# The second block's second product by seven half-size products, and a start-up that loads the second pair's v first

## The chip, the cores and the metric

The kernel runs on one core of a Trainium2 chip. Its time is the device time of one execution in microseconds (us); several executions are measured, and the median counts. A core has five engines that run their own instruction streams in order and meet at semaphores: TensorE (PE in the profile; its weight loads are PEld) multiplies matrices into the PSUM buffers, VectorE (DVE) and ScalarE (ACT) work elementwise and move PSUM to SBUF, GpSimd (POOL) works on SBUF and issues some DMAs, SyncE (SP) issues the other DMAs. DMA queues move data between HBM and SBUF.

## The reference

Two layers, one after the other, over 4 sequences of 768 tokens (3072 tokens), 8 heads of 64 dimensions:

```python
state = np.zeros((B, H, D, D))
for t in range(S):
    state = gamma * state + outer(k[:, :, t], v[:, :, t])   # per head, gamma = 1 - 2**(-5 - h)
    y[:, :, t] = scale * q[:, :, t] @ state                 # scale = 1 / sqrt(D)
x = y as [3072 tokens, 512]
h = np.maximum(x @ w_in, 0.0)                               # w_in 512 x 2048
out = (h * h) @ w_out                                       # w_out 2048 x 512
```

All inputs and the output are float32; the kernel multiplies in bfloat16 and accumulates in float32.

## The kernel before

The recurrence is done in 24 chunks of 128 tokens: scores of a chunk (queries against keys, masked), its outputs (scores against v, plus queries against the state so far), and the state carried on in PSUM. Decay is put into scaled copies of q, k and v. The first four chunks are done as two pairs (`scores_pair`, `outputs_pair`, `state_pair`, `finish_pair`): pair 0 is chunks 0 and 1, pair 2 is chunks 2 and 3. Chunks 4 to 7 go through `scale_q`, `scale_kv`, `transpose_k`, `scores`, `state`, `outputs`; from chunk 8 on a packed form with DMA transposes is used (`scores2` and so on).

The feed-forward layer works on blocks of chunks: `BLOCKS` gives the first block four chunks, and ten more blocks two chunks each. Its first product (L846, `first_product`) has 128-column weights of w_in as the stationary side; ScalarE takes the relu out of PSUM (L855), VectorE squares it (L826). For the second product there are two ways:

- the plain one (`second`, L1175, stored by L1185 and L1187): 16 matmuls of 512 columns for each chunk;
- `seven_products` (L880 for its matmuls, L876 for its sums): the block's 256 tokens, the 2048 inner values and the 512 output columns are halved each, and the product is made of seven half-size products (each eight matmuls of 256 columns) of sums s1 to s4 of parts of h and t1 to t4 of parts of w_out (L341, `sum_w_out`). Its last product, with s4, is kept back and run in the next block, between that block's units (`kept`).

Before the change blocks 2 to 10 use seven products, block 1 the plain way. Block 0 uses the plain way for its first two chunks and seven products for its last two, in `last_of_first` (L1000 for the sums, L1004 and L1039 for the matmuls). There `u` is a sum that VectorE makes from the first finished products and that must be made before the third product (s3 with t3) goes on in the same buffer; s3 is made by `third_sums`, s4 by `fourth_sums`.

Nothing is scheduled automatically. Each engine runs its instructions in the order in which the program issues them, and that order is written by hand: the start-up is a list of calls (from `keep_awake(10, ...)` to `load_kv(4, "k")`), and after it the blocks' work is cut into pieces; `put(n, what)` issues a step after piece n. Block 0's pieces are 5 to 32 (5 to 16 its first product, 17 to 32 its second), block 1's are 33 to 48, and each later block has pieces of its own after them. `attend(m, scaled, places)` puts the steps of chunk m: the scaling of q at `scaled`, then at the five places q's turning and k's scaling, k's turning, the first scores, the second scores and the state, the outputs.

In the start-up SP issues the loads in the order of the calls: q and k of the first chunks, the first pair's v, the first half of w_in's group 0, the second pair's v, the second half of w_in's group 0, and so on. Weights of w_in arrive in float32 and are cast by several engines (`cast_w`; its letters name the engines for the four parts: G is GpSimd, V VectorE, S ScalarE). `first_unit(0, 0, c, (part,))` runs half of the first product's group 0 for chunk c, eight matmuls of 128 columns. `keep_awake` runs matmuls on zeros while data is awaited.

PSUM buffers are given out by pools: `ps_f` has four buffers that are used in turn, `ps_tp`, `ps_st`, `ps_y` and `ps_c` one each. A new tile waits until the last use of the buffer's former tile is over.

Of the kernel before, what the change touches and what calls it, by code (L numbers as in the profile page):

```python
# [9 lines left out]
FP32 = mybir.dt.float32  # L10
BF16 = mybir.dt.bfloat16
# [13 lines left out]
PACK_FROM = 8  # L25


SEVEN = range(2, 11)


@with_exitstack
def kernel(
# [14 lines left out]
    C = 128  # L47
# [142 lines left out]
    load_pair(0, "kn", k, raw_k, heads_of[1])  # L190
    load_pair(2, "kn", k, raw_k)
    load_pair(0, "vn", v, raw_v)
    load_w_in(0, parts=2, between=lambda: load_pair(2, "vn", v, raw_v))
    load_w_in(1, parts=2)
    for g in range(2, NQ):
        load_w_in(g)
# [657 lines left out]
    def relu(hv, hp, on_scalar=False):  # L854
        nc.scalar.activation(hv, hp[:], AF.Relu)  # L855
        squares.append((hv, on_scalar))
# [3 lines left out]
    def seven_products(tb):  # L860
# [4 lines left out]
            t.rearrange("s p hh d -> s (p hh d)").rearrange("s (j t) -> s j t", t=C)  # L865
            for t in (k_bds[0], k_bds[1], v_bds[0])
        )
        s3 = a21
        t1, t2, t3, t4 = sums
        b11, b21, b22 = (  # L870
# [21 lines left out]

        def rest():
            first_sums(slice(4, 8))
            pa = ps_tp.tile([P, HN], FP32, name="tp")
            pb, pe, pd = (ps_f.tile([P, HN], FP32, name="psf") for _ in range(3))
            oa, ob = (opool.tile([P, DM], FP32, name="osb") for _ in range(2))
            a, u, v = (upool.tile([P, HN], FP32, name=f"u{i}") for i in range(3))
            r0 = first[tb] * C
            for js, stop in ((range(0, 6), False), (range(6, 8), True)):  # L900
                product(pa[:], a11, b11, js, True, stop)
                product(pe[:], a22, t4, js, True, stop)
                if stop:
                    nc.scalar.activation(a[:], pa[:], AF.Copy)
                yield
            add(s3, a11, a21, ALU.subtract)
            product(pd[:], s1, t1, range(8), True, True)
            yield
            add(s4, a12, s2, ALU.subtract)
            product(pb[:], s2, t2, range(8), True, True)  # L910
            add(u[:], pb[:], a[:])
            yield
            for js in (range(0, 4), range(4, 8)):
                product(pa[:], a12, b21, js, False, js[-1] == 7)
                if js[0]:
                    nc.scalar.activation(oa[:, 0:HN], pa[:], AF.Copy)  # L916
                yield
            for js in (range(0, 4), range(4, 8)):
                product(pb[:], s3, t3, js, False, js[-1] == 7)
                if js[0]:  # L920
                    add(v[:], pb[:], a[:])
                    add(ob[:, HN:DM], pd[:], v[:])
                    add(ob[:, 0:HN], pe[:], v[:])

                    def last_product():
                        product(pd[:], s4, b22, range(8), False, True)
                        add(oa[:, HN:DM], pd[:], u[:])
                        yield
                        nc.sync.dma_start(out[r0 + C : r0 + 2 * C], ob[:])
                        yield  # L930
                        nc.sync.dma_start(out[r0 : r0 + C], oa[:])
                        yield

                    kept.append(last_product())
                yield
# [167 lines left out]
    def first_unit(tb, g, c, parts=(0, 1)):  # L1103

        if tb not in h2s:
            h_tiles(tb)
        if (tb, g, c) not in open_ps:
            open_ps[tb, g, c] = ps_f.tile([P, FPQ, C], FP32, name="psf")
        hp = open_ps[tb, g, c]
        cols = slice(c * C, (c + 1) * C)  # L1110
        half = FPQ // 2
        for part in parts:
            for fq in range(part * half, (part + 1) * half):
                first_product(tb, hp[:, fq, :], g * FPQ + fq, cols)
        if 1 in parts:
            relu(h_of(tb, g * FPQ, (g + 1) * FPQ)[:, :, cols], open_ps.pop((tb, g, c)))

    def ffn_pieces(tb):
        nch = BLOCKS[tb]
        TB = nch * C  # L1120
        if tb == 0:
            first_sums, last_sums, second_products = last_of_first()
            put(11, first_sums, 0)
            put(17, first_sums, 1)
            put(26, last_sums[0])
            put(27, last_sums[1])
            for f in range(FPQ, NFB):
                hp = ps_f.tile([P, TB], FP32, name="psf")
                first_product(tb, hp[:], f, slice(0, TB))
                relu(h_of(tb, f)[:, 0], hp)  # L1130
                yield
            yield from second_products()
            return
        elif tb <= 2:

            for c in range(nch):
                for g in range(NQ):
                    first_unit(tb, g, c)
                    if c * NQ + g in (1, 2, 3) and kept:
                        next(kept[0])  # L1140
                    if c * NQ + g == 4:
                        kept.clear()
                    if tb in SEVEN and (c, g) == (1, 3):
                        first_sums, rest = seven_products(tb)
                        first_sums(slice(0, 4))
                    yield
            if tb in SEVEN:
                yield from rest()
                return
        else:  # L1150
            h_tiles(tb)
            per = 512 // TB
            if tb in SEVEN:
                first_sums, rest = seven_products(tb)
            for f0 in range(0, NFB, per):
                hp = ps_f.tile([P, per, TB], FP32, name="psf")
                for f in range(f0, f0 + per):
                    first_product(tb, hp[:, f - f0, :], f, slice(0, TB))
                relu(h_of(tb, f0, f0 + per), hp, tb in SEVEN and f0 // per in (1, 3))
                if f0 // per in (1, 2, 3) and kept:  # L1160
                    next(kept[0])
                if f0 // per == 4:
                    kept.clear()
                if f0 // per == 5 and tb in SEVEN:
                    first_sums(slice(0, 4))
                yield
            if tb in SEVEN:
                yield from rest()
                return


        def second(op, j, g, cols=slice(0, DM)):
            for fq in range(FPQ):
                f = g * FPQ + fq
                nc.tensor.matmul(  # L1175
                    op[:],
                    lhsT=h_of(tb, f)[:, 0, j * C : (j + 1) * C],
                    rhs=w_out_bf[g][:, fq, cols],
                    start=(f == 0),
                    stop=(f == NFB - 1),  # L1180
                )

        def store(op, j, cols=slice(0, DM)):
            osb = opool.tile([P, DM], FP32, name="osb")
            nc.scalar.activation(osb[:, cols], op[:], AF.Copy)  # L1185
            r0 = (first[tb] + j) * C
            nc.sync.dma_start(out[r0 : r0 + C, cols], osb[:, cols])  # L1187


        for j in range(nch):  # L1190
            op = ps_f.tile([P, DM], FP32, name="psf")
            for g in range(NQ):
                second(op, j, g)
                if g == NQ - 1:
                    store(op, j)
                yield
# [33 lines left out]
    transpose_pair_k(2, 1, *f)  # L1230
    cast_pair_v(0, 0)
    cast_pair_v(0, 1)
    mask_a = scores_pair(2, 0, (st, f), spare[:, 0:1024])
    keep_awake(2)
    end_awake()
# [4 lines left out]
    outputs_pair(0, 1)  # L1240
    mask_b = scores_pair(2, 1, (tp, f), spare[:, 1024:2048])
    mask_b(0)
    mask_b(1)
    finish_pair(0, 0)
    finish_pair(0, 1)
    state_pair(0, 1, "SV")
    cast_w("in", 0, (0,), "GGGG")
    cast_pair_v(2, 0)
    cast_pair_v(2, 1, on_scalar=True)
    first_unit(0, 0, 0, (0,))  # L1250
    first_unit(0, 0, 1, (0,))
    cast_w("in", 0, (1,), "GGVV")
    outputs_pair(2, 0, ((ps_y, "y"), st))
    outputs_pair(2, 1)
    finish_pair(2, 0)
    state_pair(2, 0, "VV")
# [23 lines left out]
    def attend(m, scaled, places):  # L1280
        if m % 2 == 0:
            put(scaled, scale_q, m, 0)
            put(scaled + 2 if m == 4 else scaled, scale_q, m, 1)
            put(places[0], transpose_q, m)
        put(16 if m == 4 else places[0], scale_kv, m)
        put(places[1], transpose_k, m)
# [27 lines left out]
    put(20, sum_w_out, 0)  # L1314
    put(22, sum_w_out, 1, (0, 1), slice(0, 2))
    put(24, sum_w_out, 1, (0, 1), slice(2, 4))
    put(26, sum_w_out, 1, (2, 3))
    attend(4, 12, (17, 19, 21, 23, 28))
    attend(5, None, (25, 28, 30, 32, 34))
    attend(6, 30, (33, 35, 37, 39, 42))  # L1320
    attend(7, None, (38, 42, 44, 46, 49))
    packed = pack_constants()
    put(27, next, packed)
    put(34, next, packed)
    for j, t in enumerate([s_bds[2]] + ks_bd2s + v_bd2s):
        for hh in range(2):
            put(35 + 2 * j + hh, zero_off_diagonal, t, hh)
# [1 line left out]
    for j, t in enumerate(k_big):  # L1329
# [5 lines left out]
    done = [57, 62] + [70 + 8 * j for j in range(14)]  # L1335

    ahead = {
        8: (37, 41, 44, 46, 48), 9: (0, 0, 49, 51, 53), 10: (50, 54, 55, 57, 60), 11: (0, 0, 60, 63, 68)
    }
    for m, d in zip(range(PACK_FROM, NCHUNK), done):  # L1340
        attend2(m, d, done[m - PACK_FROM - 1] if m > PACK_FROM else 0,
# [58 lines left out]
```

## Time and profile before

| what | value |
|---|---|
| median of 3 runs | 204.03 us (203.91 to 204.12) |
| the profiled execution | 203.7 us, its span 201.9 us |
| TensorE busy | 196.4 us, 97% of the span, 2403 matmuls |
| VectorE busy | 148.5 us, 74% |
| ScalarE busy | 127.8 us, 63% |
| GpSimd busy | 81.1 us, 40% |
| granted TensorE clock | 1.000 |
| moved by DMA | 36.57 MB |

The span runs from the first to the last instruction; the time of the execution is 1.8 us longer. The profile comes from one execution, so sums of its rows stand against 203.7 us. A row of a timeline has its start, its length (of all its instructions together), engine, line, operation, what is written and read, and the count; in brackets stands how long the engine had been idle before it and what it waited for. TensorE's instructions overlap, so the distance between starts tells what one costs.

### The profile page before, as it was taken

What the parts mean: (1) busy time and instruction counts of PE and PEld (TensorE: products, weight loads), DVE (VectorE), ACT (ScalarE), POOL (GpSimd) and SP (SyncE); (2) the same over time, 40 slices, a digit from 0 to 9 for tenths busy, and PEclk for the clock granted to TensorE, in tenths of its full rate; (3) what the DMA queues carried; (4) which work ended last, traced back from release to release, by engine and by line L of the source; (5) the groups of instructions that cost most, each with busy time, mean ns of one, the idle gap of its engine ahead of it and who ended that gap; (6) DMA issues with size and microseconds to landing.
All of it is one profiled execution on the core that took longest, in us unless ns stands there. A gap on an engine that the chain in (4) does not pass through costs nothing.

```text
span 201.9 us, 5925 instructions
## 1 busy us (share of the span) xinstructions
PE 196.4 (97%) x2403; PEld 167.2 (83%) x2408; DVE 148.5 (74%) x315; ACT 127.8 (63%) x259; POOL 81.1 (40%) x152
## 2 busy tenths in 40 slices
PE   8999999999999999999999999999999999999993
PEld 8688445669965998999999999999899999999883
DVE  3987899789684678777787777777787687485374
ACT  8775875164852766783785785783775766863730
POOL 8675721099930973362622084224382022200000
PEclk9999999999999999999999999999999999999999
DMA  5999999999799999889999789999999572200202
GB/s 171 356 371 398 337 200 196 252 246 291 201 229 234 103 137 160 153 202 201 211 183 221 134 145 167 230 178 204 178 148 167 157 107 54 109 0 3 104 3 106
DMA packets 92252, 36.57 MB, mean 181 GB/s; under 512 B 68544, under 2 KB 88256, under 8 KB 92224
## 3 DMA queue, kind: packets, MB, share of 16 engines
q1 hardware_dynamic: 77312, 32.52, 68.7%
q0 software_dynamic: 14912, 3.67, 20.6%
q8 instruction: 19, 0.31, 0.6%
q14 instruction: 9, 0.07, 0.1%
HBM read 27.26 MB, written 6.29 MB: 166 GB/s over the span
## 4 chain that ended last, share of the span: by engine, by line
PE 94%; DVE 2%; ACT 1%; issue 1%; DVEq 0%
PE psf L846 42%; PE psf L880 18%; PE tp L880 7%; PE psf L1175 3%; PE psf L1039 3%; PE y L363 3%; PE psf L1004 3%; PE st L747 2%; PE y L803 2%; PE y L796 2%; PE c_ps L774 2%; PE c_ps L642 1%; PE st L445 1%; PE y L521 1%; DVE osb L876 1%
## 5 line engine op out<-in xcount | busy, mean ns | idle before, releaser
L846 PE MATMUL psf<-xt,w_in_bf 128*128 128x256 bf16 (+2 forms) x879 | 92.3, 259 | 0.1
L846 PEld LDWEIGHTS <-w_in_bf 128*128 128x128 bf16 x880 | 71.2, 98 | 11.2
L855 ACT ACTIVATE h<-psf 128x512 bf16<-128x512 f32 x96 | 56.2, 595 | 21.2 <-PE psf L846 18.9
L725 POOL COPY v_bd<-v 64x512 bf16<-64x512 bf16 x32 | 21.5, 673 | 73.7 <-DVE v L717 64.8
L826 DVE TENSOR_TENSOR h<-h 128x512 bf16<-128x512 bf16 x80 | 33.6, 433 | 21.1 <-ACT h L855 20.5
L880 PEld LDWEIGHTS <-h 128*128 128x128 bf16 x288 | 26.5, 98 | 3.0 <-DVE h L826 0.3
L160 POOL DMA_DIRECT2D k_big<-in_k_dram x32 | 21.0, 674 | 0.0
L880 PE MATMUL psf<-w_sum,h 128*128 128x256 bf16 x136 | 19.1, 273 | 0.0
L880 PE MATMUL tp<-w_out_bf,h 128*128 128x256 bf16 x136 | 19.1, 273 | 0.0
L880 PE MATMUL psf<-w_sum,k_bd 128*128 128x256 bf16 x144 | 17.9, 273 | 0.0
L876 DVE TENSOR_TENSOR u<-psf,u 128x256 f32<-128x256 f32 x18 | 7.6, 424 | 11.3 <-PE psf L880 10.9
L880 PEld LDWEIGHTS <-k_bd 128*128 128x128 bf16 x144 | 13.8, 98 | 1.5
L783 ACT ACTIVATE s_bd<-c_ps 64x256 bf16<-64x256 f32 x29 | 10.7, 370 | 6.5 <-PE c_ps L774 6.5
L876 DVE TENSOR_TENSOR osb<-psf,u 128x256 f32<-128x256 f32 x26 | 10.3, 422 | 6.1 <-PE psf L880 5.8
L376 DVE TENSOR_TENSOR qs<-qn,qf 128x512 bf16<-128x512 f32 x20 | 14.0, 704 | 0.4 <-DMA qn<-in_q_dram 0.4
L784 ACT ACTIVATE s_bd<-c_ps 64x256 bf16<-64x256 f32 x29 | 11.0, 379 | 0.4
L754 DVE TENSOR_TENSOR pt<-st,cmask 128x512 bf16<-128x512 f32 x16 | 11.0, 688 | 0.1
L717 DVE TENSOR_TENSOR v<-stage,kf 128x512 bf16<-128x512 f32 x16 | 11.0, 684 | 0.0
L916 ACT ACTIVATE osb<-tp 128x256 f32<-128x256 f32 x8 | 3.1, 385 | 12.2 <-PE tp L880 12.2
L810 ACT ACTIVATE xt<-y 128x512 bf16<-128x512 f32 x16 | 9.6, 598 | 1.8 <-PE y L803 1.2
L824 ACT ACTIVATE h<-h 128x512 bf16<-128x512 bf16 x16 | 10.1, 630 | 0.5
L876 DVE TENSOR_TENSOR k_bd<-h 128x512 bf16<-128x512 bf16 x18 | 10.1, 559 | 0.3
(151 smaller groups left out, 304.7 us busy)
## 6 DMA issues: line engine op xcount, KB each, us to landing
qn<-in_q_dram SPq DMA_DIRECT2D x12, 512.0 KB, 5.5
out_dram<-osb SPq DMA_DIRECT2D x23, 256.0 KB, 2.8
stage<-in_v_dram SPq DMA_DIRECT2D x32, 96.0 KB, 4.5
stage<-in_moe_w_in_dram SPq DMA_DIRECT2D x4, 512.0 KB, 7.6
stage<-in_moe_w_in_dram SPq DMA_DIRECT2D x2, 1024.0 KB, 8.1
w_out_bf<-in_moe_w_out_dram POOLq DMA_DIRECT2D x4, 512.0 KB, 10.2
kn<-in_k_dram SPq DMA_DIRECT2D x6, 256.0 KB, 6.0
k_big<-in_k_dram POOLq DMA_DIRECT2D x32, 48.0 KB, 4.3
```

What stands on the lines that cost most here:

```text
L160: nc.gpsimd.dma_start(t[rows, :, p, hh, :], k[b, 2 * p + hh, (i + 3 * n) * C : (i + 3 * n + 3) * C].rearrange("(w s) d -> s w d", s=64),)
L376: engine.tensor_tensor(out=out, in0=by, in1=table[:, :, None].to_broadcast([P, H, D]), op=ALU.mult)
L717: nc.vector.tensor_tensor(out=v2.rearrange("s (u p) d -> s u p d", u=2), in0=vn, in1=kf2[:, i, :, :, None].to_broadcast([P, 2, NPAIR, D]), ...
L725: nc.gpsimd.tensor_copy(v_bd[rows, :, hh, :], v2[rows])
L754: nc.vector.tensor_tensor(out=pt[:], in0=st[:], in1=cmask2.rearrange("s r t -> s (r t)")[:, None, :].to_broadcast([P, 2 * NPAIR, C // 2]), ...
L783: nc.scalar.activation(s_bd[halves[0], :, 0, :], c[halves[0]], AF.Copy)
L784: nc.scalar.activation(s_bd[halves[1], :, 1, :], c[halves[1]], AF.Copy)
L826: nc.vector.tensor_mul(hv, hv, hv)
L846: nc.tensor.matmul(hp, lhsT=w_in_bf[g][:, cb, fq * 128 : (fq + 1) * 128], rhs=xts[tb][:, cb, cols], start=(cb == 0), stop=(cb == NCB - 1),)
L855: nc.scalar.activation(hv, hp[:], AF.Relu)
L876: nc.vector.tensor_tensor(out=out, in0=in0, in1=in1, op=op)
L880: nc.tensor.matmul(to, lhsT=left[:, j], rhs=right(j) if callable(right) else right[:, j], start=(start and j == 0), stop=(stop and j == NF ...
```

## The change

Four things change:

- `SEVEN` takes in block 1. Its sums s1, s2 and s4 lie in a tile of the `hpool` pool instead of the buffers `k_bds` and `v_bds`, which chunks 6 and 7 still use then; its buffer `pa` comes from `ps_f` instead of `ps_tp`. One of its squares goes to ScalarE. The plain second product is no longer used by any block but block 0's own form.
- In the start-up the second pair's v is loaded ahead of w_in's group 0, both of its casts go to GpSimd ahead of w_in's, the fourth cast of w_in's first half goes to VectorE between `mask_b(0)` and `mask_b(1)`, and `outputs_pair(2, 0)` is issued ahead of the two half units of the first product.
- At block 0's end the outputs of chunk 4 are issued after piece 24 instead of 28, the last of the w_out sums (into w_sum3) after piece 27 instead of 26, behind `u`; s3 and s4 one piece later (27 and 28 instead of 26 and 27), the turning of chunk 5's k one piece sooner (27 instead of 28), and chunk 6's two scalings of q at 29 and 31 instead of both at 30.
- Chunks 6 to 9 get other places for some steps, and `pack_constants` is issued after pieces 12 and 15 instead of 27 and 34.

```diff
-SEVEN = range(2, 11)
+SEVEN = range(1, 11)
...
     load_pair(0, "vn", v, raw_v)
-    load_w_in(0, parts=2, between=lambda: load_pair(2, "vn", v, raw_v))
+    load_pair(2, "vn", v, raw_v)
+    load_w_in(0, parts=2)
     load_w_in(1, parts=2)
...
+        if tb == 1:
+            room = hpool.tile([P, 4096], BF16, name="h2").rearrange("e (n j t) -> e n j t", n=4, t=C)
+            s1, s2, s4 = (room[:, n] for n in range(3))
         s3 = a21
...
-            pa = ps_tp.tile([P, HN], FP32, name="tp")
+            pa = (ps_f if tb == 1 else ps_tp).tile([P, HN], FP32, name="psf" if tb == 1 else "tp")
...
-            relu(h_of(tb, g * FPQ, (g + 1) * FPQ)[:, :, cols], open_ps.pop((tb, g, c)))
+            relu(h_of(tb, g * FPQ, (g + 1) * FPQ)[:, :, cols], open_ps.pop((tb, g, c)), (tb, c, g) == (1, 1, 2))
...
-            put(26, last_sums[0])
-            put(27, last_sums[1])
+            put(27, last_sums[0])
+            put(28, last_sums[1])
...
     cast_pair_v(0, 0)
     cast_pair_v(0, 1)
+    cast_pair_v(2, 0)
+    cast_pair_v(2, 1)
     mask_a = scores_pair(2, 0, (st, f), spare[:, 0:1024])
...
     mask_b(0)
+    cast_w("in", 0, (0,), "GGGV")
     mask_b(1)
     finish_pair(0, 0)
     finish_pair(0, 1)
     state_pair(0, 1, "SV")
-    cast_w("in", 0, (0,), "GGGG")
-    cast_pair_v(2, 0)
-    cast_pair_v(2, 1, on_scalar=True)
+    outputs_pair(2, 0, ((ps_y, "y"), st))
     first_unit(0, 0, 0, (0,))
     first_unit(0, 0, 1, (0,))
     cast_w("in", 0, (1,), "GGVV")
-    outputs_pair(2, 0, ((ps_y, "y"), st))
     outputs_pair(2, 1)
...
-            put(scaled + 2 if m == 4 else scaled, scale_q, m, 1)
+            put(scaled + 2, scale_q, m, 1)
...
-    put(26, sum_w_out, 1, (2, 3))
-    attend(4, 12, (17, 19, 21, 23, 28))
-    attend(5, None, (25, 28, 30, 32, 34))
-    attend(6, 30, (33, 35, 37, 39, 42))
-    attend(7, None, (38, 42, 44, 46, 49))
+    put(26, sum_w_out, 1, (2,))
+    put(27, sum_w_out, 1, (3,))
+    attend(4, 12, (17, 19, 21, 23, 24))
+    attend(5, None, (25, 27, 30, 32, 34))
+    attend(6, 29, (33, 35, 37, 39, 42))
+    attend(7, None, (36, 40, 43, 45, 48))
     packed = pack_constants()
-    put(27, next, packed)
-    put(34, next, packed)
+    put(12, next, packed)
+    put(15, next, packed)
...
-        8: (37, 41, 44, 46, 48), 9: (0, 0, 49, 51, 53), 10: (50, 54, 55, 57, 60), 11: (0, 0, 60, 63, 68)
+        8: (41, 45, 44, 46, 48), 9: (0, 0, 47, 51, 53), 10: (50, 54, 55, 57, 60), 11: (0, 0, 60, 63, 68)
```

## The prediction

> **What bounds the kernel now.** I read the page first, then TensorE's, VectorE's and GpSimd's timelines of the first 66 us, then the DMA view of one window. The page says which engine sets the time:
>
> ```profile
> span 201.9 us, 5925 instructions
> ...
> PE 196.4 (97%) x2403; PEld 167.2 (83%) x2408; DVE 148.5 (74%) x315; ACT 127.8 (63%) x259; POOL 81.1 (40%) x152
> ...
> PE 94%; DVE 2%; ACT 1%; issue 1%; DVEq 0%
> ```
>
> TensorE is 97% busy and carries 94% of the chain of waits, so any idle time put into its queue, or matmul time taken out of it, moves the end one for one. The busy column counts overlapping latency, so I price matmuls by the distance between starts: in a row of eight, the next row's start minus this one's. From TensorE's timeline (start, length of the row, engine, line, operation, count):
>
> ```profile
> 59.33 1.89 PE L1175 MATMUL psf<-w_out_bf,h 128*128 128x512 bf16 x8
> 61.06 0.39 PE L445 MATMUL st<-qT,k_bd 128*128 128x128 bf16 x4
> ...
> 77.34 1.04 PE L880 MATMUL psf<-w_sum,k_bd 128*128 128x256 bf16 x8
> 78.21 1.04 PE L880 MATMUL tp<-w_out_bf,h 128*128 128x256 bf16 x8
> ```
>
> A 512-column matmul is 1.73 / 8 = 0.216 us, a 256-column one 0.87 / 8 = 0.1086 us; 128 columns are 0.056 us (four of them are 0.22), and a change of matmul shape costs about 0.09.
>
> The start-up is edited too. GpSimd's timeline shows when its loads arrive (in brackets: idle before, and who ended it); the row of TensorE is the first after the second pair's outputs; the last row is from the DMA view of 11.5 to 13 us:
>
> ```profile
> 10.56 1.16 POOL L586 CAST v_bd<-vn 128x512 bf16<-128x512 f32 x2
> 11.89 1.43 POOL L351 CAST w_in_bf<-stage 128x256 bf16<-128x256 f32 x4 [0.17 <-DMA stage<-in_moe_w_in_dram]
> 14.64 0.61 POOL L586 CAST v_bd<-vn 128x512 bf16<-128x512 f32 x1 [1.31 <-DMA vn<-in_v_dram]
> 15.93 0.92 POOL L351 CAST w_in_bf<-stage 128x256 bf16<-128x256 f32 x2 [0.69 <-DMA stage<-in_moe_w_in_dram]
> ```
> ```profile
> 15.91 0.40 PE L682 MATMUL y<-qT,s_bd 128*128 128x128 bf16 x4
> ```
> ```profile
> q8 instruction: 1, 0.02, 4.0%
> ```
>
> Landings in the trace: first pair's v 10.50, first half of w_in group 0 11.84, second pair's v 14.58, w_in's second half 15.88. A w_in half takes 1.3 us; the v before took 1.5 (9.00 to 10.50), this v 2.7. The extra 1.2 begins just when one 16 KB instruction packet starts (11.92, 0.95 us long), and the next landings keep the lag: one DMA engine is that far behind.
>
> The third place is around 44 us, where VectorE's order makes TensorE wait:
>
> ```profile
> 42.40 0.72 DVE L341 TENSOR_TENSOR w_sum<-w_out_bf,w_sum 128x1024 bf16<-128x1024 bf16 x1
> 43.04 0.79 DVE L1000 TENSOR_TENSOR h<-h 128x512 bf16<-128x512 bf16 x2
> 43.86 0.42 DVE L1000 TENSOR_TENSOR u<-psf,u 128x256 f32<-128x256 f32 x1
> 44.20 0.75 DVE L1000 TENSOR_TENSOR h<-h,h 128x512 bf16<-128x512 bf16 x2
> ```
> ```profile
> 43.53 0.60 PE L1004 MATMUL psf<-w_out_bf,h 128*128 128x256 bf16 x4
> 44.34 0.60 PE L1004 MATMUL psf<-w_sum,h 128*128 128x256 bf16 x4 [0.21 <-DVE u L1000]
> 44.77 0.22 PE L445 MATMUL st<-qT,k_bd 128*128 128x128 bf16 x1
> 45.25 0.34 PE L445 MATMUL st<-qT,k_bd 128*128 128x128 bf16 x3 [0.26 <-ACT k_bd L426]
> ```
>
> By starts the losses are 44.34 - (43.53 + 0.43) = 0.37 for u, 45.25 - 44.83 = 0.42 for chunk 5's turned keys, and 0.07 before the next scores at 46.37: 0.86 in all.
>
> **Part 1, the start-up: +1.0 us.** The second pair's v now loads before w_in's first half, and outputs_pair(2, 0) stands before the two half units of the first product. By the row spacing that v lands near 12.0, its two GpSimd casts (0.6 each) end by 13.3, and the outputs run at 14.26 without a wait, in 16 x 0.017 = 0.27 (the 32 of both groups took 0.53). So TensorE asks for w_in at 14.6. But w_in's half is now the last of the same three loads: the bytes in front of it and the late engine are the same, so it lands at about 14.6, where the v landed. Three GpSimd casts (0.34 to 0.47 apart, 0.4 to 0.5 long by the rows at 11.89 and 15.93) end near 15.05, 15.4 and 15.75; after the third, 14 matmuls x 0.056 remain: 16.55. Then outputs_pair(2, 1) with its change of shape, 0.36: L682 starts at 16.9 instead of 15.91. In the next 4.6 us every TensorE row starts within 0.1 us of the one before it or of the VectorE cast that it feeds itself (17.75 for 17.81), so nothing gives it back. Ends: if w_in lands unhindered at 13.35, its casts end at 14.5, TensorE waits for nothing and saves the 0.15 it now waits for v at 15.15: -0.15 to +1.1; I take +1.0.
>
> The fourth cast goes to VectorE, between mask_b(0) and mask_b(1), and waits there for the same load: mask_b(1) moves from 13.96 to about 14.9, the state cast behind it from 14.78 to 15.6. Their readers come at 16.6 and 16.9, and wait for neither; with the load early the cast costs mask_b(1) 0.3, before a reader at 15.5. ScalarE loses a 0.63 cast, which frees nothing that is waited for.
>
> **Part 2, block 0's end: +0.4 us.** Let T be the end of the eight w_sum0 and w_sum1 matmuls. Chunk 4's outputs now come earlier, so after T TensorE has only the turn of chunk 5's keys (0.22) and eight a12 matmuls (0.87): it wants s3 and u at T + 1.09. VectorE starts u at T + 0.2 (last matmul 0.16 past its slot), then w_sum3 (0.64 to the next start) stands ahead of s3, which was done before u until now: u 0.34, w_sum3 0.64, s3's first half 0.42 plus 0.03: T + 1.63, a wait of 0.54 in u's place. Then s3 t3 (0.43), scores (0.22), s3 t3 and pe (0.87): the second scores are due at T + 3.15. They need the one st buffer, which VectorE frees by its mask: after s3's second half and s4's two (0.34 each) comes chunk 6's first scaling of q, which now stands ahead of the mask (0.60): the mask starts at T + 3.16, ends at T + 3.85, and the scores wait 0.75. So 1.29 instead of 0.86: +0.43. The ends are -0.86 (no wait left) and +0.8 (each new wait half a VectorE operation longer).
>
> **Part 3, block 1's second product: -0.84 us, less 0.1.** Out go 32 x 0.2163 = 6.92 us, in come 7 x 8 x 0.1086 = 6.08. VectorE gets four sums of 512 (0.42), two of 1024 (0.69) and five of 256 (0.42): 5.2 us; ScalarE two copies of 0.39 and a square of 0.63 for two copies of 0.60. VectorE is busy 8.18 of the 10 us from 47 to 57 and 5.52 of the 9 from 57 to 66: 5.3 free, hardly more than what comes, so a product may wait: 0 to 0.5, I take 0.1, as the sums stand half a block ahead of their products. The pa buffer in ps_f is copied out before the next block's first unit wants it.
>
> The Trainium skill speaks against this edit: "TensorE: Matmul & The Clock Gate", Back-to-back issue gap, gives 131 ns a pair of weight load and matmul at 512 columns and 81 at 128, so half-size ones would cost far more than half; by it 32 x 0.131 = 4.2 us would become between 56 x 0.081 = 4.5 and 56 x 0.131 = 7.3, a loss. The trace's 0.216 and 0.1086 disagree with it and fit the page's isolated gap of N / 2.4 + 2.5 ns.
>
> **Covered edits, at nothing.** pack_constants (GpSimd, 40.95 to 43.2) moves ahead of the fourth w_out load: issued near 28 instead of 25.7, and its turn on the queue comes at 35.83 (landings 29.11, 32.47, 35.83, 39.19); uncovered, w_sum's second part at 40.10 would wait. Chunk 8's q is scaled about 1.3 us later, and SP turns it by DMA ahead of chunk 8's keys: q landed at 66.78 and the keys at 68.09 before scores at 69.67; both shift by about 1.4 us, to 69.5, the scores by 0.7, to 70.35. That leaves 0.9.
>
> **Sum.** 1.0 + 0.43 - 0.84 + 0.1 = +0.7: 203.7 of the profiled execution becomes 204.4. The median of the runs is 0.33 above that execution, so 204.03 becomes 204.7.
>
> **Rivals.**
> - *w_in is not late* (the lag falls on another engine or later): -0.15 + 0.43 - 0.84 + 0.1 = -0.46: 203.6. For it: the lag rests on one packet. Against: TensorE's instructions up to 14.26, which I take that packet's time to follow, are unchanged. It decides from a landing before about 13.9 on: there the start-up costs 0.3 and the sum is zero. Chance 0.2.
> - *Block 0's end gains what it lost* (s3 ready by T + 1.09, mask by T + 3.15): 1.0 - 0.86 - 0.84 + 0.1 = -0.6: 203.4. Against: w_sum3's 0.64 stands in front of s3. Chance 0.08.
> - *Chunk 8's turned keys come late*, past 70.35 at L747, or VectorE's 5.2 us do not fit: 0.8 more, 205.5. Chance 0.1.
> - *Half-size matmuls bound by weight loads*: a load is 98 ns, 10 under the pitch; were the pitch 0.124, the 0.84 would be gone: 205.5. Against: some 490 such matmuls (L880) keep 0.1086. The skill's pair rule above points this way. Chance 0.02.
>
> **How the numbers follow.** Forecast 0.6. A measurement here can tell about 0.2%, 0.41 us: 203.62 to 204.44 is no change. The forecast's own spread, 204.2 to 205.2, gives 0.53 slower and 0.07 same; the first rival, astride the bound, 0.12 and 0.08; the second 0.06 and 0.02; the others are slower. Faster 0.18, same 0.17, slower 0.65. From 203.5 to 205.4 holds the forecast and most of the first and third rivals.
>
> **What would show it.** Right: GpSimd's first w_in casts near 14.6 with TensorE's first L846 row behind them at 15.1, L682 near 16.9; a wait on VectorE before s3 t3 and another before L445 near 47.5; 56 matmuls of 256 in 6.1 us; all later rows 0.7 late. Wrong: w_in cast before 14, no wait at s3 t3, or waits among the new products.

## The result, and the profile after

| | before | after |
|---|---|---|
| median | 204.06 us | 206.60 us (205.91 to 206.90, 6 runs) |
| ratio | | 1.0119, interval 1.0101 to 1.0137 |
| profiled execution, its span | 203.7, 201.9 us | 205.91, 204.1 us |

The kernel became slower by 2.5 us in the medians and by 1.2% in the ratio, more than three times the 0.7 that was forecast, and the time lies above the range. The line numbers of after lie 1 to 4 above those of before: L847 is the first product, L880 the sums of `seven_products`, L884 its matmuls, L827 the squares, L1004 and L1008 the sums and matmuls of block 0's end, L446 and L453 the scores and their mask, L748 the packed scores. The page of after shows the same busy time of TensorE in a longer span, and VectorE now in the chain of waits with 7%, where it had 2%:

```profile
span 204.1 us, 5990 instructions
PE 196.4 (96%) x2432; PEld 169.3 (83%) x2432; DVE 152.3 (75%) x326; ACT 127.5 (62%) x259; POOL 81.1 (40%) x152
...
PE 84%; DVE 7%; DMA 3%; SPq 3%; issue 1%; POOL 1%; DVEq 0%
```

**The start-up.** From the timelines of GpSimd and TensorE (start, length, engine, line, operation, count, and in brackets the idle time before it and who ended it):

```profile
12.05 1.18 POOL L587 CAST v_bd<-vn 128x512 bf16<-128x512 f32 x2 [0.29 <-DMA vn<-in_v_dram]
14.67 2.09 POOL L352 CAST w_in_bf<-stage 128x256 bf16<-128x256 f32 x5 [1.44 <-DMA stage<-in_moe_w_in_dram]
```
```profile
15.25 1.65 PE L847 MATMUL psf<-xt,w_in_bf 128*128 128x128 bf16 x16 [0.54 <-POOL w_in_bf L352]
...
17.17 0.40 PE L683 MATMUL y<-qT,s_bd 128*128 128x128 bf16 x4
```

The second pair's v landed at 12.00 and w_in's first half at 14.62, as worked out (12.0 and 14.6): the exchange of the loads moved the lag onto w_in. L683 starts at 17.17, which was 15.91 before: +1.26.

**Block 0's end.** VectorE's timeline, GpSimd's beside it, and the two TensorE rows that waited:

```profile
44.74 0.68 DVE L342 TENSOR_TENSOR w_sum<-w_out_bf,w_sum 128x1024 bf16<-128x1024 bf16 x1
45.34 0.75 DVE L1004 TENSOR_TENSOR h<-h 128x512 bf16<-128x512 bf16 x2
...
46.69 1.09 DVE L377 TENSOR_TENSOR qs<-qn,qf 128x512 bf16<-128x512 f32 x1
47.70 0.68 DVE L453 TENSOR_TENSOR pt<-st,cmask 128x512 bf16<-128x512 f32 x1
```
```profile
46.62 0.62 POOL L393 CAST v_bd<-vn 128x512 bf16<-128x512 f32 x1
```
```profile
45.81 0.61 PE L1008 MATMUL psf<-w_sum,h 128*128 128x256 bf16 x4 [0.42 <-DVE h L1004]
...
48.44 0.38 PE L446 MATMUL st<-qT,k_bd 128*128 128x128 bf16 x4 [0.91 <-DVE pt L453]
```

By starts the third product loses 0.59 (eight matmuls from 44.35 on fill 0.87, to 45.22) and the second scores 1.09 (46.48 + 0.87 = 47.35): 1.68 together instead of 0.86 before. The w_out sum stands ahead of s3 and chunk 6's scaling of q ahead of the mask, as forecast. What was not forecast is the length of that scaling at 46.69: 1.09 us where it takes 0.68 elsewhere, beside GpSimd's cast of chunk 6's v at 46.62. Before, that cast came 2.3 later and the two scalings of chunk 6's q (46.24, 1.28 together) had none beside them:

```profile
48.94 0.61 POOL L392 CAST v_bd<-vn 128x512 bf16<-128x512 f32 x1
```

GpSimd reaches it sooner in after because the work of `pack_constants`, which before ran from 40.95 to 43.2 ahead of it, has moved to an earlier place.

**Block 1's second product.** The same three timelines:

```profile
59.02 0.76 DVE L880 TENSOR_TENSOR h<-h 128x512 bf16<-128x512 bf16 x1
59.81 0.71 DVE L880 TENSOR_TENSOR h<-h,h 128x512 bf16<-128x512 bf16 x1
60.45 0.83 DVE L827 TENSOR_TENSOR h<-h 128x512 bf16<-128x512 bf16 x1
61.31 0.42 DVE L880 TENSOR_TENSOR h<-h 128x512 bf16<-128x512 bf16 x1
```
```profile
58.22 2.77 POOL L709 CAST ks_bdp<-stage 64x512 bf16<-64x512 f32 x4
```
```profile
61.33 0.39 PE L884 MATMUL psf<-w_sum,h 128*128 128x256 bf16 x2 [0.54 <-DVE h L827]
...
64.77 0.38 PE L446 MATMUL st<-qT,k_bd 128*128 128x128 bf16 x4 [0.19 <-DVE pt L453]
```

Two sums and a square of 0.42 took 0.76, 0.71 and 0.83 while GpSimd cast the keys of chunks 8 and 9; the sum after that cast took 0.42 again. The trace of before has such rows too, a square and a scaling beside GpSimd's casts of keys:

```profile
55.45 0.83 DVE L826 TENSOR_TENSOR h<-h 128x512 bf16<-128x512 bf16 x1
56.20 1.10 DVE L376 TENSOR_TENSOR ks<-kn,kf 128x512 bf16<-128x512 f32 x1
```
```profile
55.31 1.44 POOL L708 CAST ks_bdp<-stage 64x512 bf16<-64x512 f32 x2
```

In after the square came 0.70 late for its product (60.63 to 61.33 by starts), and the second scores lost 0.36 (64.41 to 64.77). So 1.06 of waits met the 0.84 that the half-size matmuls save.

From there on all rows are 2.2 late (block 3's first product at 82.76 instead of 80.54), and the later blocks have the pace of before. The sum of the profile: 1.26 + 0.82 - 0.84 + 1.06 = 2.30 against 2.21 measured.

The profiled execution of after is its fastest; the others take some 0.7 more. What those lost isn't in its trace. The traces of several experiments show where 0.2 to 1.5 us can go after block 2: TensorE waits at L748 (chunk 10's packed scores) for the DMA that turns chunk 10's keys. In after's own trace that DMA lands at 81.93, 1.7 before its reader.

### The profile page after: what moved, and what is told of

It is laid out like the page before. It is cut to its first block, busy times and chain, and to the rows that moved or that the text cites. A ratio compares the mean times of both kernels' runs of the same rounds, so it can differ in the third digit from the quotient of the medians.

```text
span 204.1 us, 5990 instructions
## 1 busy us (share of the span) xinstructions
PE 196.4 (96%) x2432; PEld 169.3 (83%) x2432; DVE 152.3 (75%) x326; ACT 127.5 (62%) x259; POOL 81.1 (40%) x152
## 4 chain that ended last, share of the span: by engine, by line
PE 84%; DVE 7%; DMA 3%; SPq 3%; issue 1%; POOL 1%; DVEq 0%
PE psf L847 41%; PE psf L884 19%; PE tp L884 7%; DMA stage<-in_moe_w_in_dram 3%; PE psf L1043 3%; SPq L115 3%; PE psf L1008 2%; PE y L804 2%; PE st L748 2%; PE y L797 2%; PE c_ps L775 2%; DVE h L880 1%; DVE qs L377 1%; DVE pt L453 1%; PE st L446 1%
## 5 line engine op out<-in xcount | busy, mean ns | idle before, releaser
L847 PE MATMUL psf<-xt,w_in_bf 128*128 128x256 bf16 (+2 forms) x880 | 92.6, 259 | 0.8 <-POOL w_in_bf L352 0.5
L847 PEld LDWEIGHTS <-w_in_bf 128*128 128x128 bf16 x880 | 71.2, 98 | 12.1 <-POOL w_in_bf L352 1.2
L827 DVE TENSOR_TENSOR h<-h 128x512 bf16<-128x512 bf16 x79 | 33.5, 437 | 20.3 <-ACT h L856 20.0
L884 PEld LDWEIGHTS <-h 128*128 128x128 bf16 x344 | 31.6, 98 | 4.4 <-DVE h L827 1.1
L884 PE MATMUL psf<-w_sum,h 128*128 128x256 bf16 x168 | 23.4, 273 | 0.6 <-DVE h L827 0.5
L884 PE MATMUL tp<-w_out_bf,h 128*128 128x256 bf16 x136 | 19.1, 273 | 0.0
L884 PE MATMUL psf<-w_sum,k_bd 128*128 128x256 bf16 x144 | 17.9, 273 | 0.0
L880 DVE TENSOR_TENSOR u<-psf,u 128x256 f32<-128x256 f32 x20 | 8.5, 423 | 11.4 <-PE psf L884 10.9
L880 DVE TENSOR_TENSOR osb<-psf,u 128x256 f32<-128x256 f32 x29 | 11.4, 420 | 6.7 <-PE psf L884 6.3
L884 PEld LDWEIGHTS <-k_bd 128*128 128x128 bf16 x144 | 13.7, 98 | 1.5
L825 ACT ACTIVATE h<-h 128x512 bf16<-128x512 bf16 x17 | 10.7, 629 | 0.5
L880 DVE TENSOR_TENSOR k_bd<-h 128x512 bf16<-128x512 bf16 x18 | 10.1, 559 | 0.3
```

The source lines that it names most:

```text
L827: nc.vector.tensor_mul(hv, hv, hv)
L847: nc.tensor.matmul(hp, lhsT=w_in_bf[g][:, cb, fq * 128 : (fq + 1) * 128], rhs=xts[tb][:, cb, cols], start=(cb == 0), stop=(cb == NCB - 1),)
L880: nc.vector.tensor_tensor(out=out, in0=in0, in1=in1, op=op)
L884: nc.tensor.matmul(to, lhsT=left[:, j], rhs=right(j) if callable(right) else right[:, j], start=(start and j == 0), stop=(stop and j == NF ...
```

## The experiments

The theory behind experiments 1 to 4: the new waits are VectorE's, because its operations take up to twice as long beside GpSimd's casts, and each of the three places costs what its rows show.

**1. The seven half-size products alone** (`seven_only`): before, with only this part of the change.

```diff
-SEVEN = range(2, 11)
+SEVEN = range(1, 11)
...
+        if tb == 1:
+            room = hpool.tile([P, 4096], BF16, name="h2").rearrange("e (n j t) -> e n j t", n=4, t=C)
+            s1, s2, s4 = (room[:, n] for n in range(3))
```

> The kernel before with the seven products for block 1 alone (its sums in their own tile, pa in the other bank, one square on ScalarE); start-up and block 0's end as before. Theory (the matmul saving is real; what ate it in the changed kernel is three VectorE sums stretched by GpSimd casts that ran beside them): before issues GpSimd's casts of chunk 8's keys at 55.3 and chunk 9's only at 67.3, so the first sums near 57 to 59 have no cast beside them, and the time falls by 0.84 less 0 to 0.3 of waits: 203.2 to 203.5. Rival (VectorE has no room for 5.2 us more whatever runs beside it): waits of about 1 us among the new products as in the changed kernel, 204.0 to 204.3.

Measured: 206.60 us, ratio 1.0129 (1.0088 to 1.0170). The product that saves 0.84 us made the kernel 2.6 slower when nothing else moved. Its waits of TensorE (engine, line, who is waited for: us in total, times, longest):

```profile
PE psf L883 <- DVE h L826: 2.0, 2, 1.5
...
PE st L747 <- DMA kT<-ks_bdp: 0.6, 1, 0.6
```

The longest is a square that VectorE makes at 60.55, read at 61.03:

```profile
56.62 1.09 DVE L376 TENSOR_TENSOR ks<-kn,kf 128x512 bf16<-128x512 f32 x1
57.64 0.68 DVE L376 TENSOR_TENSOR qs<-qn,qf 128x512 bf16<-128x512 f32 x1
60.55 0.42 DVE L826 TENSOR_TENSOR h<-h 128x512 bf16<-128x512 bf16 x1
```
```profile
61.03 0.39 PE L883 MATMUL psf<-w_sum,h 128*128 128x256 bf16 x2 [1.49 <-DVE h L826]
```

It queues on VectorE behind two scalings of chunk 8's q, a scaling of chunk 7's k that takes 1.09 beside a GpSimd cast, and a mask. The theory missed: no cast runs beside the first sums (0.42 and 0.43 from 59.75 on), and still the products wait. The rival has the kind of wait right, and not its size: 206.60 lies 2.3 above its 204.0 to 204.3. The other places that the change gives to the steps of chunks 7 to 9 are thus no trimming. From block 1's first product to block 3's it takes 35.86 us here, 34.10 in after and 33.95 before: they bring the cost of this stretch from 1.9 down to about 0.2.

**2 and 3. After with the old start-up** (`old_start`), **and with the old end of block 0** (`old_end`).

```diff
-    load_pair(2, "vn", v, raw_v)
-    load_w_in(0, parts=2)
+    load_w_in(0, parts=2, between=lambda: load_pair(2, "vn", v, raw_v))
...
-    cast_w("in", 0, (0,), "GGGV")
...
+    cast_w("in", 0, (0,), "GGGG")
```
```diff
-            put(27, last_sums[0])
-            put(28, last_sums[1])
+            put(26, last_sums[0])
+            put(27, last_sums[1])
...
-    attend(4, 12, (17, 19, 21, 23, 24))
-    attend(5, None, (25, 27, 30, 32, 34))
-    attend(6, 29, (33, 35, 37, 39, 42))
+    attend(4, 12, (17, 19, 21, 23, 28))
+    attend(5, None, (25, 28, 30, 32, 34))
+    attend(6, 30, (33, 35, 37, 39, 42))
```

> The changed kernel with the start-up of before (w_in's first half loaded ahead of the second pair's v, casts and outputs in the old order). Theory (the start-up costs what its rows show, 17.17 against 15.91 for the first L682/L683 row): 1.26 us less than the changed kernel, 205.3 in the median, w_in's first cast near 11.9 again and the second pair's v near 14.6. Rival (the later stages have slack that the late start uses up, so that a part comes back as waits): 0.3 to 0.8 us less, 205.8 to 206.3.

> The changed kernel with block 0's end as before (chunk 4's outputs after piece 28, w_sum3 after 26, s3 and s4 after 26 and 27, chunk 5's keys turned after 28, chunk 6's q scaled at 30). Theory (VectorE's new order costs 1.68 us of waits for the old 0.86): 0.8 us less than the changed kernel, 205.8 in the median, with waits of about 0.37, 0.42 and 0.07 again. Rival (the waits come from the later start, whatever the order): no gain, 206.6.

Measured: 205.14 (ratio 1.0042, 1.0017 to 1.0066) and 205.94 (1.0081, 1.0050 to 1.0113), so 1.5 and 0.7 us below after, where 1.26 and 0.8 were expected. Block 1 begins at 47.03 and 48.06 instead of 48.66. In `old_start` 1.22 of these 1.63 are there at the first L682 row (15.95 instead of 17.17). The other 0.41 is the scaling of chunk 6's q, which here is over before GpSimd casts chunk 6's v:

```profile
45.46 0.69 DVE L376 TENSOR_TENSOR qs<-qn,qf 128x512 bf16<-128x512 f32 x1
```
```profile
46.66 0.61 POOL L392 CAST v_bd<-vn 128x512 bf16<-128x512 f32 x1
```
```profile
46.81 0.38 PE L445 MATMUL st<-qT,k_bd 128*128 128x128 bf16 x4 [0.50 <-DVE pt L452]
```

The second scores lose 0.67 here (46.81, due at 45.27 + 0.87 = 46.14) and the third product 0.59: 1.26, where the prediction has 1.29. So the new order at block 0's end costs what was forecast when no cast runs beside the scaling, and the two places are not independent: the later start has moved the scaling onto the cast. In `old_end` block 1 begins 0.60 sooner, though its own start-up is 0.21 later than that of after (17.38): the order of before is worth 0.81.

**4. After with GpSimd's zeroing sooner** (`casts_sooner`): the same steps, but all zeroing of the packed buffers at one place, so that the four casts of keys behind it run from 53.4 to 56.9 instead of 58.2 to 61.0.

```diff
-            put(35 + 2 * j + hh, zero_off_diagonal, t, hh)
+            put(35, zero_off_diagonal, t, hh)
```

> The changed kernel with all ten zeroings of the packed tiles' off-diagonals issued at place 35, ahead of chunk 7's v cast on GpSimd, so that the four casts of chunk 8's and 9's keys run some 2 to 4 us sooner (about 54.5 to 57.5 instead of 58.2 to 61.0). Theory (casts beside two-source VectorE sums stretch them from 0.42 to about 0.75): the first sums near 59 to 60.4 take 0.42 each, the wait of 0.70 before the 61.33 row goes, and most of the 0.36 before scores at 64.77: 0.7 to 1.0 less, 205.6 to 205.9 in the median. Rival (the sums are stretched by something else, or VectorE is simply full): the same sums stay at 0.75 and the time at 206.6.

Measured: 204.97, ratio 1.0042 (1.0016 to 1.0068), 1.6 below after. VectorE's rows of the same three operations:

```profile
59.06 0.42 DVE L880 TENSOR_TENSOR h<-h 128x512 bf16<-128x512 bf16 x1
59.52 0.42 DVE L880 TENSOR_TENSOR h<-h,h 128x512 bf16<-128x512 bf16 x1
59.86 0.42 DVE L827 TENSOR_TENSOR h<-h 128x512 bf16<-128x512 bf16 x1
```

They have their 0.42 back, no product waits for a sum, and from block 1's start to block 3's it takes 33.07 us instead of 34.10. That shows the cause of 1.0 of the 1.06: the time at which GpSimd casts. The other 0.6 of the gain is not in the profile of this kernel, whose execution lost 1.5 at the turning of chunk 10's keys.

**5. The second product without the rest** (`parts_apart`): after with all three edits of 2, 3 and 4.

> The changed kernel with the start-up and block 0's end of before and with GpSimd's casts of chunk 8's and 9's keys moved ahead (the edits of old_start, old_end and casts_sooner together): seven products for block 1 and the later places of chunks 6 to 9 remain. Theory (the losses are three separate ones and the saving of 0.84 is real once no cast runs beside the first sums): by the rows 46.6 at block 1's first unit as before, then 33.0 us to block 3 instead of 34.0: 1.0 less than the kernel before, 203.0 to 203.2, or up to 0.7 more where TensorE still waits for chunk 10's turned keys. Rival (the earlier GpSimd casts or the shorter block bring another wait): 204.0 or more.

Measured: 203.58, ratio 0.9990 (0.9973 to 1.0008): the product alone is now even with before, not 0.8 better. Its two remaining waits:

```profile
62.43 0.38 PE L445 MATMUL st<-qT,k_bd 128*128 128x128 bf16 x4 [0.20 <-DVE pt L452]
...
81.63 0.41 PE L747 MATMUL st<-qT,kT 128*128 128x64 bf16 x8 [0.18 <-DMA kT<-ks_bdp]
```

By starts they are 0.37 and 0.34 (80.42 + 0.87 = 81.29 is when L747 was due). A third loss is too short to be listed as a wait. The two scalings of chunk 6's q take 1.70 beside the cast of chunk 6's v at 46.74, and 1.28 before without it; TensorE's turning of that q, which reads them as they come, takes 0.73 to the next row instead of 0.44:

```profile
46.37 1.70 DVE L376 TENSOR_TENSOR qs<-qn,qf 128x512 bf16<-128x512 f32 x2
```
```profile
47.62 0.90 PE L406 MATMUL tp<-ident,qs 128*128 128x128 bf16 x8
```

So up to block 3 some 0.2 of the 0.84 is left (0.84 - 0.37 - 0.29 = 0.18): from block 1's first product to block 3's it takes 33.70 us instead of 33.95. The 0.34 at L747 comes behind that, and the profiled execution is 0.2 longer than that of before. `seven_only`, where `pack_constants` stays where it was, doesn't have the third loss: 1.28 for the scalings and 0.45 for the turning.

**6. Loads out of the turning's way** (`loads_sooner`): parts_apart, with chunk 12's q load and five v loads, which SP issues right behind the turning, issued ahead of it.

```diff
-            put(d - 29, load_q, m)
+            put(56 if m == 12 else d - 29, load_q, m)
...
-        (12, "v"): [58, 59, 60, 61, 62, 64, 65, 66] + [82 + j for j in range(8)],
+        (12, "v"): [56, 56, 56, 56, 56, 64, 65, 66] + [82 + j for j in range(8)],
```

> The same as parts_apart, with the load of chunk 12's q and the first five loads of its v issued on SP ahead of the DMA that turns chunk 10's keys instead of right behind it. Theory (those transfers, 0.5 MB of q above all, share the DMA engines with the turning and make it land late, 83.0 to 84.3 against a reader at 83 to 84): the keys land within 4.5 us of the issue and TensorE does not wait at the third row of packed scores: 0 to 0.7 less than parts_apart. Rival (the turning is late by something else, GpSimd's own loads of the keys of chunks 12 to 17, or the transfer's own spread): the same time and the same spread of runs as parts_apart.

Measured: 204.11, ratio 1.0011 (0.9992 to 1.0030). The turning was issued at 76.08 and landed at 82.07, 6.0 us, against 6.2 in parts_apart (75.35 to 81.58); L747 waited 0.7. Issuing these loads ahead does not help, so the theory fell as it was put. It does not clear the loads: issued from 72.03 on, they landed between 76.97 and 79.60, and so still moved beside the turning.

**7. Where the instruction packet falls** (`packet_sooner`): before, with the 40 matmuls on zeros of the first `keep_awake` as 80 of half the width and length, so that TensorE issues more instructions before the loads.

```diff
-    keep_awake(10, pool=ps_y, name="y")
+    idle_ps.append(ps_y.tile([P, P], FP32, name="y"))
+    for _ in range(80):
+        nc.tensor.matmul(idle_ps[0][0:64, 0:64], lhsT=still[:, 0:64], rhs=still[:, 0:64], start=True, stop=True)
```

> The kernel before, with the first 40 matmuls on zeros (128 x 128 x 128) made into 80 half as wide and long, so that TensorE has fetched 80 more instructions by any later time. Theory (the 16 KB instruction packet, which follows TensorE's progress, is what makes one DMA engine 1.2 us late): the packet starts near 9.8 instead of 11.9, and the lag falls on the first pair's v, which lands near 11.7 instead of 10.5, with w_in's first half near 13.1 instead of 11.84, and the second pair's v at 14.6 as before. Rival (the lag belongs to the place in the queue): the landings stay at 10.5, 11.84 and 14.58.

Measured in one execution: 204.09, beside 204.04 of before; one execution can't tell these apart. The 16 KB packet now starts at 10.02 instead of 11.92, and w_in's first half, which loads before the second pair's v here, lands at 13.14 instead of 11.84. GpSimd's row of its casts:

```profile
13.19 1.44 POOL L351 CAST w_in_bf<-stage 128x256 bf16<-128x256 f32 x4 [1.45 <-DMA stage<-in_moe_w_in_dram]
```

The next two landings keep their times (14.61 and 15.94, before 14.58 and 15.88). So the 1.2 to 1.3 us come with the packet and stay with all loads that follow. One thing of the theory missed: the first pair's v was expected late too (11.7), and landed at 10.49 as before, 0.47 after the packet's start. In after it is alike: the packet starts at 11.50, the second pair's v lands at 12.00 as forecast, and the load behind it is late. In both the lag fell on the load after the one that was about to land. After issues the same TensorE instructions as before up to 14.26, and its packet comes 0.4 sooner; so their number is not all that sets its time.

**8. VectorE and GpSimd side by side** (`side_by_side`): 128x512 operations of both engines alone and at the same time.

> Not the layer at all: it computes nothing of the reference and stores zeros. VectorE runs sums of two bfloat16 tiles in SBUF (128 x 512), products of a PSUM tile with an SBUF one, and casts from float32, first alone and then beside eight GpSimd casts of 128 x 512 float32 to bfloat16, and at last the sums beside GpSimd memsets. Theory (GpSimd's reading and VectorE's second SBUF operand hinder each other): sums 0.42 alone, 0.7 to 0.85 beside casts, 0.42 beside memsets; the PSUM products 0.68 either way; GpSimd's casts 0.61 alone and about 0.7 beside sums. Rival (any GpSimd work slows VectorE): the memsets stretch the sums as well.

From the timeline of both engines (L58 adds two bfloat16 operands in SBUF, L62 multiplies a PSUM operand by one in SBUF):

```profile
9.69 0.41 DVE L58 TENSOR_TENSOR c<-a,b 128x512 bf16<-128x512 bf16 x1
...
11.64 5.91 POOL L80 CAST pc<-x 128x512 bf16<-128x512 f32 x8 [11.20 <-DVE x L69]
...
13.27 0.82 DVE L58 TENSOR_TENSOR c<-a,b 128x512 bf16<-128x512 bf16 x1
...
21.28 0.68 DVE L62 TENSOR_TENSOR d<-ps,b 128x512 bf16<-128x512 f32 x1
...
36.22 7.88 POOL L86 MEMSET pm<- 128x512 bf16 x12
...
37.69 0.40 DVE L58 TENSOR_TENSOR c<-a,b 128x512 bf16<-128x512 bf16 x1
```

A sum takes 0.41 alone, 0.82 beside casts, and 0.40 beside GpSimd's memsets; the product with a PSUM operand takes its 0.68 beside casts as well as alone. VectorE's float32 casts, which alternate with the sums, go from 0.41 to 0.83, and to 0.49 beside memsets. In the stretch with both one VectorE operation and one cast pass in 0.74 (5.91 / 8), so they take turns. Where VectorE alternates sums and PSUM products, the sums keep 0.41 and the casts pay: 6.88 / 8 = 0.86. The surcharge of 0.41 is that of the kernel: 0.42 becomes 0.83, 0.68 becomes 1.09. The Trainium skill has this rule ("SBUF — State Buffer", Who interferes with whom): a VectorE instruction with two inputs in SBUF contends with a GpSimd instruction that reads SBUF, not with one that only writes it, and one with at most one SBUF input does so only in a mode that uses both of VectorE's ports, which a cast can enter. These rows agree with it: sums and casts are slowed beside casts, sums keep 0.40 beside memsets, and PSUM products keep 0.68.

**9 and 10. The turning issued sooner** (`keys_sooner`), **and one scaling later as well** (`both_sooner`).

```diff
-        ... 9: (0, 0, 47, 51, 53), 10: (50, 54, 55, 57, 60), ...
+        ... 9: (0, 0, 47, 51, 50), 10: (50, 54, 54, 55, 60), ...
```
```diff
-            put(q_at + 1, scale_q, m, 1)
+            put(q_at + 2 if m == 8 else q_at + 1, scale_q, m, 1)
```

> parts_apart with two places changed: chunk 9's v is scaled at place 50 instead of 53 and chunk 10's keys are cast at 54 instead of 55 and turned at 55 instead of 57, so that GpSimd's cast of chunk 10's keys (73.94 in parts_apart, behind the copies of chunk 9's v) can begin when the state of chunk 8 has read the buffer, near 71.9, and SP issues the turning near 73.4 instead of 75.35. Theory: the turning is late because it is issued late; it lands as much sooner, near 79.5 to 80 instead of 81.58, the scores at 81.3 wait for nothing, and the 0.35 us that they lose in parts_apart's profile are gone: 203.0 to 203.3 where parts_apart gave 203.58. Rival: the turning is held up by what else moves at that time, so it lands near 81.6 whenever it is issued (6 us in parts_apart, 3.9 in the kernel before), and the time stays 203.6.

> keys_sooner with the second scaling of chunk 8's q one place later (43 instead of 42), so that it stands behind a sum and the mask of chunk 7's first scores on VectorE (in parts_apart the two scalings take 1.28 us from 59.77 on and the mask ends at 62.38, for which the second scores wait 0.36 us at 62.43). Theory: the mask ends 0.64 us sooner, the second scores start at 62.07, and every later row 0.36 us sooner: 0.36 below keys_sooner, 202.7 to 202.9 if the keys' turning is no longer late. Rival: the scaling then stands in front of the next sum, and a product waits for that instead: the same time as keys_sooner.

Measured: 203.28, ratio 0.9973 (0.9964 to 0.9982), and 203.22, ratio 0.9964 (0.9952 to 0.9976), beside 203.92 of before on that chip. GpSimd's cast of the keys and TensorE's scores in `keys_sooner`:

```profile
72.31 1.42 POOL L708 CAST ks_bdp<-stage 64x512 bf16<-64x512 f32 x2
```
```profile
80.76 0.40 PE L747 MATMUL st<-qT,kT 128*128 128x64 bf16 x8
```

The turning was issued at 73.75 and landed at 77.87, 2.9 before its reader, which waits for nothing. It landed 3.7 sooner for an issue 1.6 sooner, so the rival (it lands at the same time anyhow) fell. The mask's wait shrank to 0.2 as well (62.09 for 61.88): GpSimd's casts of keys ended 0.4 sooner in this execution, and the first sum for block 1's second product, which stands ahead of the mask on VectorE, took 0.43 where parts_apart has 0.83 at 57.31:

```profile
57.37 0.43 DVE L879 TENSOR_TENSOR h<-h 128x512 bf16<-128x512 bf16 x1
```

In `both_sooner` that wait is gone and the next product waits 0.2 instead (63.16 for 62.95); from 60.6 on both take 4.06 us to block 2. There the rival was right: the two kernels are the same. Both are faster than before, by 0.6 to 0.7 in the medians, and in `keys_sooner` block 3 begins 0.65 sooner (79.89 for 80.54). This is not simply 0.84 less the mask's 0.2, since the 0.29 at the turning of chunk 6's q is lost here too. What makes up for it is two gaps of before that are not there: 0.24 ahead of the plain product's L1175 at 63.80 and 0.18 ahead of L880 at 76.12.

## Why the prediction came out wrong in size

- **Sign, and the mechanisms of parts 1 and 2: right.** w_in late by the swap; s3 behind the w_out sum; chunk 6's scaling ahead of the mask; half-size matmuls at 0.1086 (62.01 to 62.88 for eight in after). The first two rivals and the one by weight loads did not occur.
- **"Part 3 ... less 0.1": the step that failed.** It set VectorE's free 5.3 us against 5.2 us of new work and took 0.1 of a span "0 to 0.5". The new operations were priced at 0.42 and 0.69 whatever GpSimd did, and the free time was counted over the whole stretch. The waits were 1.06: the prices held only where GpSimd does not cast beside them (`casts_sooner`, `side_by_side`), and the trace of before had rows that show it (55.45 and 56.20). That free time over a stretch says little of a single product is what `seven_only` adds: its products wait 2.0 with no cast beside the new sums. These 0.96 are the largest of the three misses (0.96, 0.39 and 0.26).
- **"Part 2 ... +0.43": mis-sized, +0.82.** 0.05 of it is s3; 0.34 the mask, since the scaling took 1.01 to the next start and not 0.60. `old_start`, where the scaling has no cast beside it, loses the 1.26 that fit the forecast. The term at fault is "Covered edits, at nothing": it asked whether `pack_constants` stays covered at its new place, and not what GpSimd would do sooner at the old one. Chunk 6's v was cast at 46.62 instead of 48.94. The upper end, half an operation for each wait (+0.8), is just passed.
- **"Part 1 ... +1.0": mis-sized, +1.26.** The landing was right. GpSimd's casts ended 0.13 later (15.19, 15.54, 15.88), the first at 0.52 beside VectorE's new cast; and the change of shape ahead of the pair's outputs cost another 0.1. The prediction also took the packet's time to be fixed by TensorE's instructions; it came 0.4 sooner, and w_in was late all the same.
- **Third rival, half right.** VectorE's work did not fit. Turned keys did come late, but chunk 10's, in the experiments' traces, not chunk 8's.
- **The range** added the misses as if each came alone: its parts' own upper ends make 1.1 + 0.8 - 0.84 + 0.5 = 1.56, or 205.6, above the 205.4 where it stops. Two of the three terms had one cause, and they erred together.

Still open: why the turning of chunk 10's keys takes 4.1 us in one kernel and up to 7.6 in another (`casts_sooner`, 76.70 to 84.25). That the timed runs of after lost their 0.7 there is likely by the other kernels' traces, and not shown.

## What to carry to other kernels

Before work is put into an engine's free time, price it by the rows that run beside the same neighbours, not by the mean row: here a GpSimd cast could double a VectorE sum of two SBUF operands, and moving the casts by 5 us was worth more than the matmuls saved. Work that is taken out of an engine's queue brings forward what stood behind it: look at what that now runs beside. A product that needs less of the bound engine and more of a second one is only worth what the second one's queue lets through: alone it cost 2.6 us, with the neighbours moved it brought 0.6. A DMA whose reader stands some 6 us behind its issue can set the end too; issue it as soon as its source is written.

## What the runs showed of the hardware

- One 16 KB instruction packet made one load 1.2 to 1.3 us late, and all that follow kept the lag; with 40 matmuls more ahead of it on TensorE it came 1.9 us sooner (10.02 for 11.92, one execution).
- A GpSimd cast and a VectorE operation that reads two SBUF operands take turns, 0.41 us dearer for VectorE at 512 columns (0.42 to 0.83, 0.68 to 1.09). Where VectorE alternates such sums with PSUM products, it is GpSimd's cast that pays (0.86). Sums beside memsets, and PSUM products, keep their time.
- The DMA that turns chunk 10's keys, a 128x1024 tile, took 3.9 to 7.6 us from issue to landing, with the same bytes in every kernel; chunk 9's, of the same size, took 3.0 in after.
